# Moving first-layer weights and sums by one 64-byte line, and the attention products to between high and low parts

## The chip, the cores and the metric

The kernel runs on one core of one Trainium2 chip. The time is device microseconds of one execution; a profile is one further execution, recorded by the hardware profiler.

## The reference

Four batches of eight heads of attention over 768 positions with 64 elements each. A query sees the 8 first positions and the 96 before it, with a slope per head times the distance as bias. The result, 3072 rows of 512, goes through a layer of 2048 and back:

```python
scores = scale * np.matmul(q, k.transpose(0, 1, 3, 2)) + bias
a = softmax(np.where(keep, scores, -1e9))
x = np.matmul(a, v).transpose(0, 2, 1, 3).reshape(B * S, H * D)
h = x @ w_in                                    # 512 -> 2048
g = np.where(h > 0, h, np.exp(np.minimum(h, 0)) - 1)
return g @ w_out                                # 2048 -> 512
```

`w_in` and `w_out` come as 64-bit numbers.

## The kernel before, in words

The 3072 rows are taken as 12 groups of 256. Every number of the two layers is held as a high and a low part in the type fp32r, and a product is made of three: high by high, high by low, low by high. Weights are turned from 64-bit words into such parts once (`weight`), and stay in SBUF: `w0..` are the first layer's, `w1..` the second's, 16 pieces of 4096 bytes in a partition each. The inputs of a group are `xh` and `xl`, two pieces each.

Groups 0 to 2 go through the layers in four turns of four pieces while the weights arrive, group 3 in one turn (`moe`, lines 842 to 926). There an *up* of a piece is 12 matmuls of 256 columns (line 856; the weights are the stationary operand, the inputs the moving one), and a *down* is six of 512 columns (line 885; the values `gh`, `gl` are stationary, the second-layer weights move).

Groups 4 to 11 go through `seven` (lines 699 to 840). It takes two pieces together as a round: 24 up matmuls (line 713), and instead of eight products of quarter matrices in the down seven, by Strassen's scheme in Winograd's form: 21 matmuls of 256 columns (line 769). Three of the seven use values as they are, the *parts* `rh` (high) and `rl` (low); four use differences, the *sums* `sh` and `sl`. They are stationary; second-layer weights move, or mixtures of them (`mix`) that `prepare` made and stored in DRAM and that each round loads again. The down of a round is put into the plan as four pieces (`put`): parts with `rh` (6 matmuls), parts with `rl` (3), and the sums in two.

The attention of groups 3 to 11 is made by *visits* (`visit`, lines 614 to 640), four in each group for two heads each. One visit gives TensorE two things in one piece: products of weights and values of the visit two before (`values`, line 611, 48 matmul records) and the scores of a new one (`scores`, line 475, 16 records). Between them softmax runs on VectorE and ScalarE, and the transposed weights go through DRAM.

The order of the instructions of each engine is made by a planner (`Plan.order`): of what is ready it takes the smallest due time. `build` gives every piece its due time; rounds follow each other by 2 x `STEP`. `visit` passes a slack, `LATER`, by which the planner holds it back behind its operands. Addresses come from the order in which tiles are first asked for: `places_in_sbuf` asks for all places of the pool `m` in the order of `PLACES`, and weights get theirs in the pool `w` in the order in which the plan first loads them.

Of the kernel before, what the change touches and what calls it, by code (L numbers as in the profile page):

```python
# [8 lines left out]
F32 = mybir.dt.float32  # L9
# [7 lines left out]
P = 128  # L17
NG = 8
NL = P - NG
NT = 2  # L20
# [193 lines left out]
def act(n, psum=False, extra=0.0):  # L214
    return (("ACT", (55 if psum else 97) + 0.834 * n + extra, False),)


def dve(n, fast=False, port=False):
    return (("DVE", (75 + 0.521 * n) if fast else (70 + 1.042 * n), fast or port),)


def pool(n, two=True):
    return (("POOL", (30 + 2.58 * n) if two else (50 + 1.1 * n), True),)


def sp():
    return (("SP", 450.0, False),)
# [19 lines left out]
class Kernel:  # L247
# [366 lines left out]
    def visit(self, k, due):  # L614


        nc, p, N = self.nc, self.plan, len(self.fars)
        reads, cost = [], 250.0
        new = old = None
        if k < N:  # L620
            new = self.far(*self.fars[k][:-2], due, *self.fars[k][-2:])
            self.open.append(new[2])
            reads += [new[0]]
            cost += 575.0
        if k >= self.BEHIND:
            old = self.open[k - self.BEHIND]
            reads += old[0]
            cost += 640.0
        ss = [self.bank("s", "s", [P, NT, 2 * P]) for _ in range(2)]

        def both(e):
            if old:
                self.values(old[0], ss)
            if new:
                self.scores(new[0], ss, range(NT))

        p.add((("PE", cost, False),), both, reads, ss, due, slack=self.LATER)
        after = self.seat(old, ss) if old else ()
        if new:
            new[1](ss, after)  # L640
# [58 lines left out]
    def seven(self, rows, xh, xl, dues, step, last):  # L699

        nc, p, M = self.nc, self.plan, self.DM // 2
# [86 lines left out]
        for j in range(self.NFC // 2):  # L788
            d = dues[2 * j]
# [2 lines left out]
            combine(j, d + 2 * step)  # L792
            down(j, d + 3.7 * step)
        end = dues[self.NFC - 1] + 3 * step
        ob = [self.sb("io", "ob", [P, 2, M], slots=None if last else ["io0", "io1"]) for _ in range(NT)]
        lo, hi = ob
        P_ = lambda n: acc[self.OF[last][n][0]]
        q = lambda n: lambda: P_(n).t[:, self.OF[last][n][1]]
# [12 lines left out]

        if last:
            one, four, both = (self.sb("e", x, [P, M]) for x in ("one", "four", "both"))
            ob += [self.sb("io", "ob", [P, 2, M])]
            end_ = ob[2]
            p.add(act(M, True), lambda e: nc.scalar.copy(one.t, q(1)()), [P_(1)], [one], end - 9000)
            p.add(act(M, True), lambda e: nc.scalar.copy(four.t, q(4)()), [P_(4)], [four], end - 8999)
            whole = lambda x: lambda: x.t
            add(hi, 0, whole(one), q(2), [one, P_(2)])
            store(1, 0)  # L820
            add(end_, 1, whole(one), q(6), [one, P_(6)])
            p.add(dve(M), lambda e: nc.vector.tensor_tensor(both.t, end_.t[:, 1], q(7)(), ALU.add), [end_, P_(7)], [both], end - 9000)
            right = add(lo, 1, whole(both), q(5), [both, P_(5)])
            p.add(pool(M), lambda e: nc.gpsimd.tensor_tensor(lo.t[:, 0], both.t, four.t, ALU.add), [both, four], [lo], end - 9000, beside=[right])
            store(0, None)
            add(end_, 1, o(end_, 1), q(5), [end_, P_(5)])
            add(end_, 1, o(end_, 1), q(3), [end_, P_(3)])
            store(1, 1, 2, True)
            return
# [12 lines left out]
    def moe(self, rows, xh, xl, f0, f1, dues, step, part, X, last):  # L842
        nc, p, NFC, ws = self.nc, self.plan, self.NFC, self.ws
# [54 lines left out]
        for i in range(NT):  # L898
            if f1 < NFC:
                a = acc[i][0][0]  # L900
                if f0 == 0 or resumed:

                    self.parted.append(p.add(act(self.DM, True), lambda e, i=i, a=a: self.copy(e, part[i].t, a.t), [a], [part[i]], end - 9000))
                else:
                    p.add(dve(self.DM), lambda e, i=i, a=a: nc.vector.tensor_tensor(part[i].t, a.t, part[i].t, ALU.add),
                          [a, part[i]], [part[i]], end - 9000)
                continue

            for c, (a, at) in enumerate(acc[i]):
                n = at.stop - at.start  # L910
                ob = self.sb("io", "ob", [P, n], slots=None if last else ["io0", "io1"])
                e = "DVE" if c + 1 < len(acc[i]) else "ACT"
                cost = act(n, True) if e == "ACT" else dve(n)
                if f0 == 0 or resumed:
                    p.add(cost, lambda e, ob=ob, a=a, n=n: self.copy(e, ob.t, a.t[:, :n]), [a], [ob], end - 9000)
                else:
                    p.add(dve(n), lambda e, i=i, ob=ob, a=a, at=at: nc.vector.tensor_tensor(ob.t, a.t, part[i].t[:, at], ALU.add),
                          [a, part[i]], [ob], end - 9000)
                queue = nc.scalar if c else nc.sync
                k = 2 if i == 0 and 0 <= rows // W - self.HALVED[0] < self.HALVED[1] else 1  # L920

                def store(e, i=i, ob=ob, at=at, queue=queue, k=k):
                    for r in range(0, P, P // k):
                        queue.dma_start(self.out[rows + i * P + r:rows + i * P + r + P // k, at], ob.t[r:r + P // k])

                p.add((("ACT", 450.0, False),) if queue is nc.scalar else sp(), store, [ob], [], end, nbytes=P * n * 4)

    def places(self, n, x, c):

        if n == self.NE:  # L930
            return [self.THIRD[x + c]]
        return [f"{x}{n if n < self.NE else n % 2 ^ 1}{c}"]

    def build(self):
# [7 lines left out]
        at, start, wdue, dues = self.T0, {}, {}, []  # L942
        first = {}
        for n, f0, f1 in segs:
            start.setdefault(n, at)
            d, at0 = {}, at
# [8 lines left out]
        for n, (b, gi) in enumerate(groups):  # L955
# [6 lines left out]
            for hp in range(self.NP):  # L962
                d = lo + (hp + 1) * (hi - lo) / self.NP
                if len(self.EARLY) <= n < 3:
                    d = start[n] - self.SOON[0] - (self.NP - 1 - hp) * self.SOON[1]
# [5 lines left out]
        for far in soon:  # L971
            todo.append((min(far[-2], start[far[0] * self.GB + far[1]] - 1.0), lambda far=far: self.soon(far)))
        for k in range(len(self.fars) + self.BEHIND):
            d = self.fars[max(0, k - self.BEHIND)][-2] - max(0, self.BEHIND - k) * self.AHEAD
            todo.append((d, lambda k=k, d=d: self.visit(k, d)))
        for fc, d in wdue.items():
            for which in range(2):
# [15 lines left out]
        for j in range(NFC // 2):  # L993
            d = [x for (n, _, _), x in zip(segs, dues) if n == self.SE - 1][-1][2 * j + 1] + 2 * self.STEP
# [3 lines left out]
        for _, f in sorted(todo, key=lambda x: x[0]):  # L998
# [4 lines left out]

    LATE, FIRST_LOADS = 12, 22
    RESUMED = 4
    PLACES = (("pa0", 2048), ("pa1", 2048), ("pa2", 2048), ("pa3", 2048), ("pa4", 2048), ("pa5", 2048), ("qk0", 2496), ("xh0a", 2048), ("xh0b", 2048),
# [5 lines left out]
    PREPARE, SE = (168000.0, 9000.0, 6000.0), 4  # L1012
    OF = ({1: (0, 0), 2: (0, 1), 6: (1, 0), 5: (1, 1), 3: (2, 0), 7: (2, 1), 4: (3, 0)}, {1: (0, 0), 4: (0, 1), 6: (1, 0), 7: (2, 0), 2: (3, 0), 5: (4, 0), 3: (5, 0)})
# [16 lines left out]
    NEAR = {}  # L1030
    WARM = True
    WIDE, BEHIND_UP = ["h0", "h1", "v0", "t0"], 3.0
    THIRD = {"xha": "x0", "xhb": "ph2", "xla": "rk0", "xlb": "va0"}
    SLOTS = {"qk": ["rqv0", "qk0"], "v": ["va1", "va2"], "u": ["rk0", "va0"], "s": ["s0", "s1"], "t": ["t0"], "pv": ["v0", "t0"], "h": ["h0", "h1"], "o0": ["o0"], "o1": ["o1"],
             "pr": ["pr0", "pr1", "pr2", "pr3"], "tr": ["pt0", "pt1"], "pt4": ["ph0", "ph1"], "dd": [f"dd{i}" for i in range(4)], "st": [f"st{i}" for i in range(6)], "pt": ["pt0", "pt1"],
             "x": ["x0"], **{x + c: [f"{x}{n}{c}" for n in range(3)] for x in ("xh", "xl") for c in "ab"}, "e": ["e0", "e1"], "gh": ["gh0", "gh1", "gh2"],
             "gl": ["gl0", "gl1", "gl2"], "io": ["io0", "io1", "io2", "io3"], "part": [f"pa{i}" for i in range(6)], "mix": [f"pa{i}" for i in range(6)],  "hl": ["xh0a", "xh0b"], "tf": ["tf0", "tf1", "xl0a", "xl0b"],
             "g": ["io2", "io3"], "sum7": ["ph2", "x0"], "rh": ["gh0", "gh1"], "rl": ["gl0", "gl1"], "sh": ["xh2a", "xl2a"], "sl": ["xh2b", "xl2b"], "o2": ["v0"], "o3": ["t0"], "o4": ["s0"], "o5": ["s1"]}

    SOONER = {  # L1040
# [73 lines left out]

    def places_in_sbuf(self):
        for tag, size in self.PLACES:
            self.m.tile([P, size // 4], F32, tag=tag, name=self.n("place"))

    def gate(self, op):

# [249 lines left out]
```

## Time and profile before

| | us |
|---|---|
| median of 3 runs (lowest, highest) | 635.47 (634.56, 636.06) |
| the profiled execution | 634.52 |
| its span, first to last instruction | 632.7 |
| TensorE busy in it | 621.9 |

The span is what the trace shows; 1.8 us of the profiled execution lie around it. Busy TensorE is not TensorE at its peak: matmuls overlap, so the pace is read from pieces of a known number of matmuls in the chain of waits, which gives each piece the time until the next one ends.

### The profile page before, as it was taken

Reading aid. Unit: us, or ns where it says so; the run is one execution under the profiler, and the core shown is the slowest. Engines: PE = TensorE matmul, PEld = TensorE weight load, DVE = VectorE, ACT = ScalarE, POOL = GpSimd, SP = SyncE. Lnnn points to the kernel's source line nnn. Section 1 sums busy time; section 2 is a strip of 40 time slices with the busy share of each in tenths; the row PEclk is TensorE's granted clock in tenths of the full one; section 3 lists DMA queues with packets and bytes.
Section 4 is the critical chain, followed back from the end, with each engine's and each line's share of the span. In section 5 each row is a group of like instructions: output and inputs, shape, how many; then the busy total and the mean of one; then the engine's idle time right before and its main releaser. Section 6 shows DMA issues by size and latency. Waiting matters only on the chain.

```text
span 632.7 us, 19150 instructions
## 1 busy us (share of the span) xinstructions
PE 621.9 (98%) x7046; PEld 576.7 (91%) x7046; DVE 487.8 (77%) x1630; ACT 428.3 (68%) x1246; POOL 207.7 (33%) x491
## 2 busy tenths in 40 slices
PE   8999999999999999999999999999999999999995
PEld 5778888898898889999999999999999999999995
DVE  6899888878786877777877877877877877875755
ACT  5999778888656755667667667667667666655552
POOL 3645465656464784112112112112112112110000
PEclk9999999999999999999999999999999999999999
DMA  8979835322354899998898898998997997994542
GB/s 306 383 274 408 318 129 137 114 68 88 89 199 155 268 301 271 304 273 266 280 271 252 266 272 276 280 272 259 274 276 249 279 282 250 261 247 153 183 151 87
DMA packets 131171, 149.82 MB, mean 237 GB/s; under 512 B 63616, under 2 KB 82816, under 8 KB 131072
## 3 DMA queue, kind: packets, MB, share of 16 engines
q1 hardware_dynamic: 130784, 148.41, 74.9%
q8 instruction: 57, 0.93, 0.6%
q14 instruction: 42, 0.34, 0.2%
q10 hardware_dynamic: 288, 0.13, 0.1%
HBM read 117.57 MB, written 30.93 MB: 235 GB/s over the span
## 4 chain that ended last, share of the span: by engine, by line
PE 92%; DVE 3%; ACT 2%; issue 1%; DMA 1%; POOL 0%; ACTq 0%; DVEq 0%; POOLq 0%
PE h L713 28%; PE o L769 25%; PE h L856 13%; PE o L885 13%; PE s L611 5%; PE s L475 4%; PE pv L508 2%; PE t L528 1%; PE t L530 1%; DMA n_raw<-in_n_dram 1%; PE none L1141 1%; ACT pt L304 0%; ACT pr L465 0%; DVE g L397 0%; DVE hl L673 0%
## 5 line engine op out<-in xcount | busy, mean ns | idle before, releaser
L581 POOL TENSOR_SCALAR pr<-pr,st 128x168 f32<-128x168 f32 x144 | 74.1, 515 | 254.0 <-DVE st L483 197.5
L713 PE MATMUL h<-xh,w 128*128 128x256 f32 x1024 | 138.8, 278 | 0.0
L713 PEld LDWEIGHTS h<-xh,w 128*128 128x128 f32 x1024 | 127.7, 188 | 0.3
L723 DVE SCALAR_TENSOR_TENSOR gg<-e,h 128x256 f32<-128x256 f32 x128 | 53.6, 418 | 83.6 <-ACT e L722 83.5
L465 ACT ACTIVATE pr<-pr,nmax 128x168 f32<-128x168 f32 x192 | 82.8, 432 | 25.0 <-DVE nmax L463 24.7
L856 PEld LDWEIGHTS h<-xh,w 128*128 128x128 f32 x512 | 76.0, 188 | 9.8 <-DVE gl L312 0.6
L721 ACT ACTIVATE e<-h 128x256 f32<-128x256 f32 x128 | 49.0, 383 | 52.3 <-PE h L713 52.3
L885 PE MATMUL o<-w,gh 128*128 128x512 f32 x256 | 80.4, 399 | 0.4 <-ACT o L304 0.4
L856 PE MATMUL h<-xh,w 128*128 128x256 f32 x512 | 80.2, 282 | 0.2 <-DVE gl L312 0.2
L713 PE MATMUL h<-xl,w 128*128 128x256 f32 x512 | 79.8, 278 | 0.0
L713 PEld LDWEIGHTS h<-xl,w 128*128 128x128 f32 x512 | 68.3, 188 | 0.5 <-issue 0.2
L312 POOL TENSOR_TENSOR w<-g,w 128x256 fp32r<-128x256 f32 x64 | 50.2, 807 | 41.2 <-ACT w L304 20.5
L304 ACT CAST sh<-sum 128x512 fp32r<-128x512 f32 x64 | 39.9, 623 | 34.2 <-DVE sum L737 34.2
L463 DVE CUSTOM_DVE_ANT_0 pr<-s,far 128x168 f32<-128x168 f32 x192 | 53.5, 321 | 2.3 <-PE s L475 0.8
L722 ACT ACTIVATE e<-e 128x256 f32<-128x256 f32 x128 | 53.3, 416 | 2.8
L304 ACT CAST rh<-gg 128x384 fp32r<-128x384 f32 x64 | 33.0, 515 | 27.7 <-DVE gg L723 27.6
L586 DVE STREAM_TRANSPOSE tr<-pr 128x192 f32<-128x192 f32 x144 | 51.2, 366 | 0.5 <-POOL pr L581 0.3
L769 PE MATMUL o<-mix,sh 128*128 128x256 f32 x256 | 51.1, 281 | 0.0
L769 PE MATMUL o<-w,sh 128*128 128x256 f32 x256 | 50.6, 287 | 0.0
L312 DVE TENSOR_TENSOR sl<-sum,sh 128x512 fp32r<-128x512 f32 x64 | 43.7, 682 | 7.1 <-ACT sh L304 7.1
L885 PEld LDWEIGHTS o<-w,gh 128*128 128x128 f32 x256 | 42.9, 189 | 6.6 <-ACT o L304 0.8
L885 PE MATMUL o<-w,gl 128*128 128x512 f32 x128 | 45.0, 396 | 0.0
(141 smaller groups left out, 1390.7 us busy)
## 6 DMA issues: line engine op xcount, KB each, us to landing
mix<-mixed SPq DMA_DIRECT2D x192, 256.0 KB, 3.8
qk<-in_qkv_dram SPq DMA_DIRECT2D x48, 312.0 KB, 4.0
v<-in_qkv_dram SPq DMA_DIRECT2D x36, 384.0 KB, 4.8
dd<-tr SPq DMA_DIRECT2D x36, 384.0 KB, 4.1
pt<-dd SPq DMA_DIRECT2D x72, 192.0 KB, 4.0
bits<-in_w_in_dram SPq DMA_DIRECT2D x16, 512.0 KB, 7.6
bits<-in_w_out_dram SPq DMA_DIRECT2D x16, 512.0 KB, 9.4
mixed<-mix SPq DMA_DIRECT2D x32, 256.0 KB, 3.7
```

Of the source, the lines that this page charges most:

```text
L304: self.nc.scalar.copy(out, x)
L312: self.on(e).tensor_tensor(out, x, y, ALU.subtract)
L463: first = p.add((("DVE", 85 + 1.042 * LW, False),), lambda e: nc.vector.tensor_tensor_reduce(x(), s.t[:, i, :LW], tab, -(2.0 ** -(h + 1)), ...
L465: p.add(act(LW, extra=200), lambda e: nc.scalar.activation(x(), x(), AF.Exp, bias=nm, scale=-1.0, accum_out=st.t[:, n, 0:1]), [pr], [pr, s ...
L581: nc.gpsimd.tensor_scalar(pr.t[:, :LW], pr.t[:, :LW], st.t[:, n, 3:4], 1.0, ALU.mult, ALU.mult)
L586: nc.vector.transpose(tr.t[:, :, i, j], pr.t.rearrange("p (b r) -> p b r", r=32))
L713: nc.tensor.matmul(h.t, w1.t[:, s, cc * P:(cc + 1) * P], self.chunk(x, cc), start=n == 0 and s == HI and cc == 0, stop=n == 1 and cc == se ...
L722: p.add(act(W), lambda e: nc.scalar.activation(ex.t, ex.t, AF.Exp, scale=-1.0), [ex], [ex], d - 8000)
L723: p.add(dve(W), lambda e: nc.vector.scalar_tensor_tensor(gs(), ex.t, -1.0, h.t, ALU.add, ALU.max), [h, ex], [g], d - 8000)
L769: nc.tensor.matmul(acc[bank].t[:, half], a, b.t[:, LO if t == 1 else HI, x], start=j == 0 and t == 0 and n in first, stop=j == self.NFC // ...
L856: nc.tensor.matmul(h.t, w1.t[:, s, cc * P:(cc + 1) * P], self.chunk(x, cc), start=n == 0 and cc == 0, stop=n == 2 and cc == self.NCC - 1)
L885: nc.tensor.matmul(o.t[:, :at.stop - at.start], g.t[:, i * P:(i + 1) * P], w2.t[:, s, at], start=fc == f0 and n == 0 and s == HI and not r ...
```

## The change

Three things change. All weights are now asked for in `places_in_sbuf`, second-layer ones first, then a place of 64 bytes that nothing uses, then first-layer ones, then the other tiles in a new order. The sums move from `xh2`, `xl2` to `io0` to `io3`, and the values `gg` and the output tiles of the last part go the other way. With that the places start on other 64-byte lines; counted modulo four:

| operand | role in the matmul | line before | line after |
|---|---|---|---|
| first-layer weights `w0` | up, stationary | 2 | 3 |
| inputs `xh`, `xl` | up, moving | 1 | 2 |
| parts `rh`, `rl` (and `gh`, `gl`) | down, stationary | 1 | 1 |
| sums `sh`, `sl` | down, stationary | 1 | 3 |
| second-layer weights `w1` | down, moving | 2 | 2 |
| mixtures `mix` | down, moving | 2 | 2 |

All slices of these tiles that a matmul reads begin a multiple of 512 bytes from the start, so each keeps its tile's line.

Second, a visit whose values are for group 5 or later gets a due time counted back from the start of that group, two rounds from one visit to the next, half a unit behind the high parts of a down and half before the low ones. Third, such visits have a smaller slack.

```diff
@@ visit
-        p.add((("PE", cost, False),), both, reads, ss, due, slack=self.LATER)
+        p.add((("PE", cost, False),), both, reads, ss, due, slack=self.LATER if k < self.NP * 2 else self.LATER - 2500.0)
@@ seven
-        ob = [self.sb("io", "ob", [P, 2, M], slots=None if last else ["io0", "io1"]) for _ in range(NT)]
+        ob = [self.sb("io", "ob", [P, 2, M], slots=self.OUT + (["xh2a", "xl2a"] if last else [])) for _ in range(NT)]
...
-            ob += [self.sb("io", "ob", [P, 2, M])]
+            ob += [self.sb("io", "ob", [P, 2, M], slots=self.OUT + ["xh2a", "xl2a"])]
@@ moe
-                ob = self.sb("io", "ob", [P, n], slots=None if last else ["io0", "io1"])
+                ob = self.sb("io", "ob", [P, n], slots=self.OUT if f0 == 0 else ["io0", "io1"])
@@ build
         for k in range(len(self.fars) + self.BEHIND):
+            b, gi, hp = self.fars[max(0, k - self.BEHIND)][:3]
             d = self.fars[max(0, k - self.BEHIND)][-2] - max(0, self.BEHIND - k) * self.AHEAD
+            n = b * self.GB + gi
+            if n > self.SE:
+                d = start[n] - 2.3 * self.STEP + 0.5 - 4 * self.STEP * (self.NP - 1 - hp)
             todo.append((d, lambda k=k, d=d: self.visit(k, d)))
@@ the places
-    PLACES = (("pa0", 2048), ("pa1", 2048), ("pa2", 2048), ("pa3", 2048), ("pa4", 2048), ("pa5", 2048), ("qk0", 2496), ("xh0a", 2048), ("xh0b", 2048),
...
+    PLACES = (("w10", 4096), ("w11", 4096), ("w110", 4096), ("w111", 4096), ("w112", 4096), ("w113", 4096), ("w114", 4096), ("w115", 4096),
+             ("w12", 4096), ("w13", 4096), ("w14", 4096), ("w15", 4096), ("w16", 4096), ("w17", 4096), ("w18", 4096), ("w19", 4096), ("wline16", 64),
...
+    OUT = ["xh2b", "xl2b"]
...
-             "g": ["io2", "io3"], "sum7": ["ph2", "x0"], "rh": ["gh0", "gh1"], "rl": ["gl0", "gl1"], "sh": ["xh2a", "xl2a"], "sl": ["xh2b", "xl2b"], "o2": ["v0"], "o3": ["t0"], "o4": ["s0"], "o5": ["s1"]}
+             "g": ["xh2a", "xl2a"], "sum7": ["ph2", "x0"], "rh": ["gh0", "gh1"], "rl": ["gl0", "gl1"], "sh": ["io0", "io1"], "sl": ["io2", "io3"], "o2": ["v0"], "o3": ["t0"], "o4": ["s0"], "o5": ["s1"]}
@@ places_in_sbuf
-            self.m.tile([P, size // 4], F32, tag=tag, name=self.n("place"))
+            (self.w if tag[0] == "w" else self.m).tile([P, size // 4], F32, tag=tag, name=self.n("place"))
```

TensorE's order before, in `seven`, in front of the first products of a visit (the names are tiles, `s` the bank that a visit fills, `pt` and `v` its weights and values):

```order
L769 MATMUL o_7118<-w_113_982,rl_7086 128x256
L769 MATMUL o_7119<-mix_6956,rl_7086 128x256
L769 MATMUL o_7137<-mix_6987,sh_7082 128x256 x2
L769 MATMUL o_7137<-mix_6987,sl_7094 128x256
L769 MATMUL o_7137<-w_107_830,sh_7082 128x256 x2
L769 MATMUL o_7137<-w_107_830,sl_7094 128x256
L611 MATMUL s_7154<-pt_1322_7016,v_6750 64x64
```

Here the visit stands between the two puts of sums. The same place of TensorE's order now, in front of a visit:

```order
L713 MATMUL h_7281<-xl_6302,w_339_1454 128x256 x2
L713 MATMUL h_7281<-xl_6698,w_339_1454 128x256 x2
L769 MATMUL o_7203<-w_119_1170,rh_7250 128x256 x2
L769 MATMUL o_7203<-w_125_1261,rh_7250 128x256 x2
L769 MATMUL o_7204<-mix_7135,rh_7250 128x256 x2
L611 MATMUL s_7318<-pt_1334_7168,v_6920 64x64
```

It has moved from behind some of the sums to behind the high parts. And behind the visit, now:

```order
L475 MATMUL s_7319<-qk_6899 64x168
L769 MATMUL o_7203<-w_119_1170,rl_7269 128x256
L769 MATMUL o_7203<-w_125_1261,rl_7269 128x256
L769 MATMUL o_7204<-mix_7135,rl_7269 128x256
L769 MATMUL o_7226<-mix_7162,sh_7267 128x256 x2
L769 MATMUL o_7226<-mix_7162,sl_7277 128x256
L769 MATMUL o_7226<-w_119_1170,sh_7267 128x256 x2
```

The three matmuls of the low parts come first there, then all twelve of the sums; before, some or all of the sums were left.

## Rows read from the trace of the kernel before

**Rows 1.** The page, parts 1 and 2: busy time of the engines, and TensorE's granted clock.
```profile
PE 621.9 (98%) x7046; PEld 576.7 (91%) x7046; DVE 487.8 (77%) x1630; ACT 428.3 (68%) x1246; POOL 207.7 (33%) x491
...
PEclk9999999999999999999999999999999999999999
```

**Rows 2.** Busy time by stage: PE, PEld, DVE, ACT, POOL, clock, DMA share, GB/s.
```profile
75.00:245.00 170.00, 169.37 (x1542) 150.28 (x1541) 137.53 (x379) 123.58 (x354) 107.47 (x193) 1.00 0.53 165
245.00:620.00 375.00, 375.00 (x4611) 364.15 (x4610) 280.31 (x990) 237.63 (x680) 62.31 (x215) 1.00 0.85 255
```

**Rows 3.** Chain of waits, 410 to 470 us: start, length, engine, line, matmuls.
```profile
433.75 2.73 PE h L713 x24
436.48 2.38 PE o L769 x21
438.86 2.83 PE h L713 x24
441.69 2.47 PE o L769 x21
444.17 2.73 PE h L713 x24
446.90 1.70 PE o L769 x15
...
450.03 0.91 PE o L769 x6
450.94 2.73 PE h L713 x24
...
456.12 1.61 PE o L769 x12
457.74 2.73 PE h L713 x24
```

**Rows 4.** The same view, 254 to 272 us: visits at two other places.
```profile
255.03 0.68 PE o L769 x6
...
257.14 1.97 PE o L769 x15
259.11 2.73 PE h L713 x24
...
264.22 0.94 PE h L713 x8
...
266.60 2.04 PE h L713 x16
268.63 2.38 PE o L769 x21
```

**Rows 5.** Chain of waits, first and last of the slow pieces of 24.
```profile
271.02 2.83 PE h L713 x24
...
613.16 2.83 PE h L713 x24
```

**Rows 6.** Groups of instructions, shapes kept apart: form and count, busy us, mean ns.
```profile
L885 PE MATMUL o<-w,gh 128*128 128x512 f32 x256 | 80.4, 399 | 0.4 <-ACT o L304 0.4
L856 PE MATMUL h<-xh,w 128*128 128x256 f32 x512 | 80.2, 282 | 0.2 <-DVE gl L312 0.2
...
L885 PE MATMUL o<-w,gl 128*128 128x512 f32 x128 | 45.0, 396 | 0.0
L856 PE MATMUL h<-xl,w 128*128 128x256 f32 x256 | 40.4, 280 | 0.0
```

**Rows 7.** Chain of waits between 75 and 245 us.
```profile
88.55 1.83 PE o L885 x8
...
231.10 0.91 PE h L856 x8
...
232.93 0.47 PE h L856 x4
...
233.86 0.93 PE h L856 x8
```

11 rows, old and new, of the table PLACES are left out of this document.

## The prediction, made before the result was known

> **What bounds the kernel now.** [...] Busy time by stage shows where it is less than full: from 75 to 245 us it is busy 169.37 of 170 us, and from 245 to 620 us all of 375.00 [rows 2]. So in the long last stage no wait counts, and only the pace at which TensorE passes from one matmul to the next can change the time. What is left is before 75 us and in the last 12 us, where this change moves no instruction of TensorE.
>
> The chain of waits then gives that pace, and it shows two. In this stage the work comes in rounds: 24 up matmuls (line 713) and 21 down matmuls (line 769), all of one form, 256 columns. Some pieces of 24 take 2.73 us and others 2.83; pieces of 21 take 2.38 or 2.47 [rows 3]. Per matmul that is 113.6 ns against 117.8, a difference of 4.2 ns, with the same shape, clock and count and no idle time between them. I call them the fast and the slow rhythm. Three rules can be read from the same rows. First, the rhythm changes only at two kinds of place. Second, from a down piece to the next up piece it always changes over (2.38 then 2.83, 2.47 then 2.73), and from up to down it never does. Third, after attention products (lines 611 and 475) that stand inside a down piece the rest of that piece is slow: the 6 that follow take 0.91 us where 6 of the fast rhythm take 0.68 [rows 3, 4]. The slow tail of 6 then changes over into a fast piece of 24. One further case stands in the trace: attention products inside an up piece, after 8 of its 24; the 16 left take 2.04 us and the down piece after them is fast (2.38) [rows 4]. There the rhythm came out fast without a change-over.
>
> What do these places have in common? The up matmuls hold first-layer weights in the array and stream inputs; the down matmuls hold parts or sums and stream second-layer weights. By the addresses, both streams change their 64-byte line at each passage between up and down: weights start on line 2 of every four, inputs, parts and sums on line 1. In an up matmul the held operand is one line behind the streamed one (+1), in a down matmul one under (-1).
>
> [...]
>
> **The change part by part.** *The work.* TensorE gets the same instructions. Eight input scalings go from ScalarE to GpSimd and three subtractions from GpSimd to VectorE. From 245 us on, VectorE is busy 280 of 375 us, ScalarE 238 and GpSimd 62 [rows 2]; that cover hides these edits, and I cost them at nothing. Were the cover gone, they would show as idle time of TensorE, of which there is none now.
>
> *The lines.* After the change everything streamed starts on line 2 of four (inputs, second-layer weights, mixed weights), first-layer weights and sums on line 3, parts on line 1. So up matmuls and the 12 sum matmuls of a down piece are at +1, the 9 part matmuls at -1, and the parity of neither stream changes any more, at any passage.
>
> *What the rhythm costs now.* Slow in this stage are 17 up pieces of 24 (the first at 271.02, the last at 613.16), the 17 pieces of 21 behind them, and the tails after attention products: 18 of 6, 6 of 12 and one of 15 [rows 3 to 5]. 17 x 0.10 + 17 x 0.09 = 3.2 us, and (18 x 6 + 6 x 12 + 15) x 4.2 ns = 0.8 us. So the rhythm can give back 4.0 us here and no more. Of each 180 matmuls (four rounds, 23.99 us with two visits, 433.75 to 457.74 [rows 3]) 63 are slow.
>
> *The places of attention.* Visits now stand one and three rounds apart; after the change every two rounds, always after the 6 high-part matmuls of a down piece, with the 3 low-part matmuls behind. That place occurs once in the trace: 6 in 0.68 us, then the products, then 15 in 1.97 us, then a fast 2.73 [rows 4]. 15 of the fast rhythm take 1.70 [rows 3], so entry and slow tail cost 0.27, and 0.23 at the usual place (0.91 - 0.68). Taking away 4.2 ns for each slow matmul (0.06 and 0.03) leaves 0.20 to 0.21 for the entry at either. The number of visits stays, so moving them costs nothing by itself. A wait is not added: the values that a visit needs come from two visits before, after the change some 23.7 us earlier (twice two rounds of 5.11 us and 1.6 us of a visit); today one round and three together give 23.99 [rows 3]. What is queued behind a late visit would be the whole of TensorE.
>
> *Which rhythm follows.* No row has sums at +1 behind parts at -1. The bounds: every matmul of the stage slow costs 117 of each 180 x 4.2 ns = 0.49 us, some 16 times, 7.9 us more; every one fast gives 4.0 us. Within these I take what the nearest rows say: entry into parts at -1 is slow, as in all rows; passing from -1 to +1 turns slow into fast (0.91 or 1.97, then 2.73); at +1 the rhythm, once fast, stays so for 24 matmuls and more. What then happens where fast up matmuls at +1 pass to parts at -1 is bounded by nothing lost (the passage keeps the rhythm now) and all 9 part matmuls of each round slow: 64 rounds x 9 x 4.2 ns = 2.4 us. At the first end only 3 low-part matmuls after each of some 30 visits are slow, 0.4 us, and the stage gains 4.0 - 0.4 = 3.6; at the other it gains 4.0 - 2.4 = 1.6. The rows do not choose; I take 2.8, a little above the middle, since no passage from up to down in the rows loses the rhythm.
>
> *The stage from 75 to 245 us.* Up matmuls (line 856, 768 of them) and down matmuls of 512 columns (line 885, 384) [rows 6] stand mixed there, mostly 8 or fewer at a time, and the up ones have both rhythms as well: 4 in 0.47 us is 117.5 each, 8 in 0.91 is 113.8. Eight down ones take 1.83 us, 229 each [rows 7]; what the rhythm costs them I can't read from pieces so short, and I let the up ones stand for both. Here up stays at +1 and down at -1, only the change of parity goes. Where the pattern is regular, 4 of 12 up matmuls of a piece are slow [rows 7]. Taken for the whole stage, all fast would gain 768 x 4/12 x 4.2 ns = 1.1 us, and all slow would lose 768 x 8/12 x 4.2 ns = 2.2 us; no row lies nearer to one end than to the other; I take zero.
>
> **The sum.** 2.8 us less. The profiled execution took 634.52 us (632.7 of it the span, 1.8 around it), which becomes 631.7; it lies 0.95 us under the median of the runs, 635.47, so I forecast 632.7.
>
> **Rivals.**
> *The change-over goes on (slower).* The rhythm turns over once in every round whatever the lines, because it hangs on the passage itself, or because parts-to-sums takes the place of down-to-up as passage from -1 to +1. For it: in the rows it never fails, in either direction. Then visits every two rounds make it worse: slow after a visit, fast for one round (45), slow for the next (45). 90 of 180 slow instead of 63 is 27 x 4.2 ns = 0.113 us, 16 times 1.8 us: 637.3. It decides from the point where more than 35% of the matmuls are slow. Against it: the up piece after the visit at 264 came out fast without any passage [rows 4]. [...]
>
> *The slow rhythm is never left.* If only parity makes the change-over, it is gone, and every visit enters by the slow way: 7.9 us more, 643.4. For it: a tail after a visit stays slow for as long as 15 matmuls [rows 4]. Against it: today's -1 and +1 differ (one passage changes over, the other does not), which parity alone does not explain.
>
> *It gives and takes.* The last stage gains only 1.6 us and the stage before loses that much or up to 2.2: 635.5 to 636.1, no change that a measurement tells. For it: both ends are bounds of rows read above. Against it: the two would have to meet at their worst ends.
>
> **How the numbers follow.** The forecast (fast from the sums on) gets 0.47, its own range 630 to 634.3, from the two ends of the parts' price and half of the bounds of the stage before. The change-over that goes on gets 0.22, never leaving the slow rhythm 0.13, give and take 0.18. The range should hold eight in ten: from 629, the forecast with all parts fast and most of the gain of the stage before, up to 640, which takes in the change-over and a part of the way to the all-slow case, which is left out. About 0.2% (1.3 us) is what a measurement of this kernel can tell from no change. Faster by that: the forecast save its weak end, 0.45. Slower: the two slow cases, 0.34 of 0.35. Within: the rest, 0.21.
>
> **What would show it.** Right: in the chain of waits after 245 us, 24 up matmuls at 2.73 us nearly everywhere, no piece of 2.83, visits at equal distances, and TensorE busy without a gap. Pieces of 21 at 2.38 mean that parts keep the rhythm, about 2.42 that they lose it. Wrong: pieces of 2.73 and 2.83 in turn (the change-over goes on), or 2.83 throughout; or idle time of TensorE before line 611 (values late) or before line 713 at the start of a group, whose last visit now lies one round before it.

## The result, and the profile after

The changed kernel takes 642.47 us (median of 9 runs, 638.47 to 645.15) against 634.80 us (9 runs beside them, 634.39 to 636.06): ratio 1.0108, with a 95% interval from 1.0082 to 1.0134. It is slower, where 632.7 us was forecast, and outside the range that was given. The profiled execution took 641.95 us, 640.2 of it the span, 7.5 more than before.

Busy time first, from the page and by the same stages as [rows 1, 2] (PE, PEld, DVE, ACT, POOL, clock, DMA share, GB/s):

```profile
PE 624.8 (98%) x7046; PEld 577.3 (90%) x7046; DVE 489.4 (76%) x1633; ACT 427.6 (67%) x1238; POOL 200.0 (31%) x496
```
```profile
75.00:245.00 170.00, 169.35 (x1540) 149.44 (x1539) 137.92 (x384) 123.47 (x354) 105.21 (x191) 1.00 0.53 167
245.00:620.00 375.00, 370.48 (x4554) 358.32 (x4553) 277.57 (x977) 234.07 (x664) 57.04 (x222) 1.00 0.90 252
```

The stage from 75 to 245 us is as before, and the clock is full in both. From 245 us on TensorE, which had no gap there [rows 2], is idle for 4.5 of 375 us, and the share of the DMA engines rises from 0.85 to 0.90 while the rate falls from 255 to 252 GB/s. So the DMA engines are occupied longer for no more bytes.

What does TensorE wait for? The waits of TensorE name one tile that they did not name before (us in total, times, longest), and the view of that tile from 245 to 600 us has the time that its loads take from issue to landing:

```profile
PE s L611 <- DMA pt<-dd: 4.4, 9, 1.0
```
```profile
DMA to landing us min/median/max: 4.0/6.2/8.9
```

The same row of the kernel before reads:

```profile
DMA to landing us min/median/max: 3.2/4.1/7.4
```

`pt` holds the turned softmax weights, which go from SBUF to DRAM (`dd`) and come back in two loads (line 597). They take 2.1 us longer at the median, and TensorE stands still until some of them have landed. The chain of waits shows it at one place. Before, it ran over TensorE alone from 410 to 470 us [rows 3]; now it leaves TensorE (start, length, what):

```profile
508.94 4.24 DMA dd<-tr
...
514.19 7.23 DMA pt<-dd
...
521.56 0.86 PE s L611 x43
...
525.63 8.90 DMA pt<-dd
...
534.67 0.86 PE s L611 x43
...
536.16 1.92 PE o L769 x15
538.09 2.72 PE h L713 x24
540.81 2.38 PE o L769 x21
...
548.02 1.97 PE o L769 x15
549.99 2.83 PE h L713 x24
552.81 2.42 PE o L769 x21
555.23 2.72 PE h L713 x24
```

In these two visits 43 of the 48 products wait until the second load of `pt` has landed (521.56 and 534.67). The pieces from 548.02 on answer to [rows 3]. The visit ahead of them had nothing to wait for, and behind it the rhythm is slow for 15 down matmuls, 24 up matmuls (2.83) and the next 9 parts (2.42 instead of 2.38), then fast up to the next visit: 48 of 90 matmuls. From a down piece to an up piece the rhythm no longer turns over. Behind the late visit at 534.67 the pieces are fast at once. They are also fast behind nine others of the eleven late visits of this stage, and slow behind the one at 521.56.

How the 7.5 us add up: I take from the trace, for each line, the sum of the times from the start of an instruction to the start of the next one on TensorE. For lines 611 and 475 (visits) it grows from 61.6 to 68.8 us. For lines 713 and 769 (the rhythm) it falls from 337.9 to 337.3. For lines 856 and 885 (most of it from 75 to 245 us) it goes from 184.4 to 184.7. The visits cost 7.2 us, the rhythm gives back 0.6. What is left, about half a microsecond, lies in the first 75 us. In these sums a wait counts for the line that stands ahead of it: 1.2 us of the rhythm's 337.3 are TensorE waiting ahead of late visits. Without them the rhythm gives back 1.8 us, and it does so because late visits mostly leave the fast rhythm behind them: of 2880 matmuls of lines 713 and 769, 795 start 116 to 123 ns before the next one, against 1079 before.

### The profile page after: what moved, and what is told of

It reads as the page before. It is cut to its first block, busy times and chain, and to the rows that moved or that the text cites. A ratio compares the mean times of both kernels' runs of the same rounds, so it can differ in the third digit from the quotient of the medians.

```text
span 640.2 us, 19191 instructions
## 1 busy us (share of the span) xinstructions
PE 624.8 (98%) x7046; PEld 577.3 (90%) x7046; DVE 489.4 (76%) x1633; ACT 427.6 (67%) x1238; POOL 200.0 (31%) x496
## 5 line engine op out<-in xcount | busy, mean ns | idle before, releaser
L581 POOL TENSOR_SCALAR pr<-pr,st 128x168 f32<-128x168 f32 x144 | 66.0, 458 | 265.4 <-DVE st L483 259.2
L463 DVE CUSTOM_DVE_ANT_0 pr<-s,far 128x168 f32<-128x168 f32 x192 | 55.6, 326 | 4.6 <-ACT xh L304 2.1
L586 DVE STREAM_TRANSPOSE tr<-pr 128x192 f32<-128x192 f32 x144 | 48.9, 358 | 0.5 <-POOL pr L581 0.3
L769 PE MATMUL o<-w,sh 128*128 128x256 f32 x256 | 47.0, 277 | 0.0
```

What stands on the lines that cost most here:

```text
L463: first = p.add((("DVE", 85 + 1.042 * LW, False),), lambda e: nc.vector.tensor_tensor_reduce(x(), s.t[:, i, :LW], tab, -(2.0 ** -(h + 1)), ...
L581: nc.gpsimd.tensor_scalar(pr.t[:, :LW], pr.t[:, :LW], st.t[:, n, 3:4], 1.0, ALU.mult, ALU.mult)
L586: nc.vector.transpose(tr.t[:, :, i, j], pr.t.rearrange("p (b r) -> p b r", r=32))
L769: nc.tensor.matmul(acc[bank].t[:, half], a, b.t[:, LO if t == 1 else HI, x], start=j == 0 and t == 0 and n in first, stop=j == self.NFC // ...
```

## The experiments

Theory A: the lines do set where the rhythm turns, and the loss comes from the new places of the visits, which make `pt` late. The rivals: the lines themselves cost time, they are without effect, or `pt` is late for another reason. All results, with the sums of starts over the whole trace in us (each ratio is to runs of the kernel before taken beside that kernel, with medians from 634.80 to 635.23 us; waits ahead of a visit or inside a down piece stand in the rhythm's sum, in e7 some 11 us):

| kernel | median us | ratio to before (95%) | visits (611, 475) | rhythm (713, 769) |
|---|---|---|---|---|
| before | 634.80 | | 61.6 | 337.9 |
| changed | 642.47 | 1.0108 (1.0082 to 1.0134) | 68.8 | 337.3 |
| e1: new lines alone | 634.76 | 0.9993 (0.9983 to 1.0003) | 61.6 | 337.9 |
| e2: new visits alone | 645.56 | 1.0157 (1.0111 to 1.0202) | 69.2 | 339.7 |
| e5: changed, mixtures later | 635.81 | 1.0017 (1.0004 to 1.0030) | 61.6 | 338.1 |
| e7: e5, visits in the sums | 642.84 | 1.0090 (1.0060 to 1.0121) | 62.7 | 347.8 |
| e8: e5, visits ahead of the parts | 631.43 | 0.9938 (0.9922 to 0.9955) | 61.8 | 333.8 |
| e8b: e8, mixtures half as late | 631.76 | 0.9951 (0.9933 to 0.9970) | 61.6 | 333.9 |
| e9: e5, parts on line 3 | 634.63 | 0.9990 (0.9981 to 1.0000) | 61.5 | 337.8 |
| e10: e8 with the old lines | 636.35 | 1.0018 (1.0008 to 1.0028) | 62.3 | 339.2 |
| e11: visits ahead of the parts alone | 634.92 | 0.9992 (0.9979 to 1.0005) | 65.4 | 334.3 |

**e1 and e2: the two halves of the change.** e1 takes back the visits' rule, e2 the places:

```diff
# e1, from the changed kernel
-            if n > self.SE:
-                d = start[n] - 2.3 * self.STEP + 0.5 - 4 * self.STEP * (self.NP - 1 - hp)
...
-slack=self.LATER if k < self.NP * 2 else self.LATER - 2500.0)
+slack=self.LATER)
# e2, from the changed kernel (not printed): PLACES, the slots and places_in_sbuf of the kernel before
```

> The changed kernel with its places in SBUF, but the products of attention where they stood before (one and three rounds apart, inside the 12 sum matmuls or between parts and sums). Theory A (lines set the rhythm, the new places of attention make the loss): TensorE doesn't wait before line 611, whose starts sum to 27 us again; down-to-up passages no longer change the rhythm, so pieces of 24 at 2.73 us nearly everywhere and a time of 630.5 to 633 us. Theory B (the new lines themselves cost time, or the slow rhythm is not left after products inside the sums): pieces of 2.83 in many rounds, 637 us or more. Theory C (lines are without effect): as before, 634 to 636 us.

> The kernel before with its places in SBUF, and only the products of attention moved to every second round, after the 6 high-part matmuls. Theory A (the new places make the values late): TensorE waits before and inside line 611 for tile pt as in the changed kernel (starts of line 611 sum to 32 to 34 us against 27.2), and the rhythm changes over once a round with slow entry at each visit, so about half of the matmuls are slow: 641 to 644 us. Theory B (the layout makes the loss): 634 to 636 us, no wait before line 611.

e2 came out at 645.56 us, with the wait before line 611 (4.0 us in 6 waits) and 31 of 62 pieces of 24 slow, as theory A expected; its time lies 1.6 us above the range given. e1 came out at 634.76 without such a wait. The loss belongs to the visits; their due time and their smaller slack were not taken apart. But e1's time is not theory A's either: it is that of "lines are without effect". Its chain of waits shows that the new places have one:

```profile
307.05 2.72 PE h L713 x24
309.77 1.02 PE o L769 x9
...
312.23 1.61 PE o L769 x12
313.83 2.83 PE h L713 x24
316.66 2.42 PE o L769 x21
319.08 2.72 PE h L713 x24
321.80 2.38 PE o L769 x21
324.18 2.72 PE h L713 x24
```

No passage from down to up turns the rhythm (2.42 then 2.72, 2.38 then 2.72; before: 2.38 then 2.83 [rows 3]). The turn to fast has moved into the down piece: 2.42 is 9 slow parts and 12 fast sums. But a visit inside the sums does not go over into the fast rhythm, as theory A had it. Behind fast matmuls (1.02 for 9) it leaves the slow rhythm (1.61 for 12, then 2.83) until the next passage from parts to sums, up to 45 matmuls later (theory B's second reason, without its time). That the gain and the cost are equal, 337.9 us in both sums, is chance: they come from different matmuls.

**e5: the mixtures behind `pt`.** The planner's start of a load of mixed weights is put back by 3 us; TensorE's order stays, but for nine matmuls of one down piece.

```diff
# the ends of the two lines
-  [self.mixed[j][n]], [x], d - 6000 - 10 * n, nbytes=P * M * 8)
+  [self.mixed[j][n]], [x], d - 6000 - 10 * n, nbytes=P * M * 8, slack=10000.0)
```

> The changed kernel; only the planner takes the loads of mixed weights as able to start 3 us later after their place is free, so that SyncE issues the two loads of pt ahead of most of them; the order of TensorE stays. Theory A (pt is late because it queues behind loads of mixed weights): line 611 back to 27 to 28 us, landing of pt 4 to 5 us against 6.3, and 635.5 to 638 us (642.5 less 6.3 us, a little given back because visits that came late had started in the fast rhythm). Theory B (the scores, the softmax or the first store to memory make it late): line 611 stays above 32 us, 641 to 643 us.

635.81 us, no wait for `pt` before line 611, the visits' sum at 61.6 again. SyncE's issues show the difference. In the changed kernel, between the store of `dd` and the loads of `pt`:

```profile
508.94 0.37 SPq L590 DMA_DIRECT2D dd<-tr  x1
510.00 0.33 SPq L557 DMA_DIRECT2D v<-in_qkv_dram  x1
511.10 0.59 SPq L752 DMA_DIRECT2D mix<-mixed  x1
511.79 0.38 SPq L549 DMA_DIRECT2D qk<-in_qkv_dram  x1
512.26 0.86 SPq L752 DMA_DIRECT2D mix<-mixed  x2
513.26 1.50 SPq L597 DMA_DIRECT2D pt<-dd  x2
```

The same in e5:

```profile
503.22 0.37 SPq L590 DMA_DIRECT2D dd<-tr  x1
504.28 0.33 SPq L557 DMA_DIRECT2D v<-in_qkv_dram  x1
504.92 0.33 SPq L549 DMA_DIRECT2D qk<-in_qkv_dram  x1
507.86 1.28 SPq L597 DMA_DIRECT2D pt<-dd  x2
509.26 2.72 SPq L752 DMA_DIRECT2D mix<-mixed  x5
```

In the changed kernel three mixtures (256 KB each) and the loads of the visit (`v`, 384 KB, and `qk`, 312 KB) stand between the store and `pt`; in e5 the mixtures follow it here, and elsewhere mostly one of them or none is left ahead. But the mixtures are not what the change brought in. The kernel before issues three of them at this point too, at each of its 27 visits from 250 us on, and in 25 of these nothing else:

```profile
506.80 0.37 SPq L590 DMA_DIRECT2D dd<-tr  x1
509.48 1.68 SPq L752 DMA_DIRECT2D mix<-mixed  x3
511.29 1.31 SPq L597 DMA_DIRECT2D pt<-dd  x2
```

What came in is `v` and `qk`, which the new visits put there as well; taking the mixtures away makes up for it. From the issue of the store to the landing of the second load of `pt` the trace has 9.6 us at the median before, 12.7 in the changed kernel and 9.8 in e5. From that landing to the first product of the visit 2.8 to 5.5 us are left before, and 1.1 to 4.9 in e5; in the changed kernel it is 2.5 us at most, and the latest load lands 0.9 us after the visit has begun. The row of landings in e5:

```profile
DMA to landing us min/median/max: 3.3/5.0/7.9
```

That is not the 4.1 us of before, but it is enough. Theory A holds, with `v` and `qk` beside the mixtures: 6.7 us between the two medians (5.8 by the two ratios) are `pt` behind other loads. To put `v` and `qk` behind `pt` instead was not tried. How loads issued ahead of `pt` make it land later is not shown: the landings of the changed kernel and e5 (6.2 and 5.0 us) go with what is issued ahead of it, but before, `pt` stood behind three mixtures too and landed in 4.1.

**e7: visits in the sums.** e5 and `+ 2.5` for `+ 0.5` in the visits' due time, so that they stand after 6 of the 12 sums.

> As the one with later mixed weights, and the products of attention of every second round stand after 6 of the 12 sum matmuls (+1 line) instead of after the 6 high-part matmuls (-1). Theory A (entry at +1 goes over into the fast rhythm after a few matmuls and no passage is left that changes it): nearly all pieces of 24 take 2.73 us, no wait before line 611, 630.5 to 633 us. Theory B (each visit enters the slow rhythm wherever it stands, and it lasts for a round): 636 to 638 us.

642.84 us (639.06 to 646.39): both missed. The mixtures now came late, the first row of TensorE's waits:

```profile
PE o L769 <- DMA mix<-mixed: 7.8, 11, 2.0
```

For the rhythm only undisturbed visits count, and they do as in e1: slow behind the visit, through the 24 up matmuls (2.83) and the parts (2.42), then fast. The first half of theory A is refuted a second time: an entry at +1 is no better.

**e8, e8b, e10 and e11: visits ahead of the parts.** By what is left of theory A a visit should stand just ahead of parts, so that the passage to the sums comes 9 matmuls later. e8 is e5 with

```diff
-                d = start[n] - 2.3 * self.STEP + 0.5 - 4 * self.STEP * (self.NP - 1 - hp)
+                d = start[n] - 2.3 * self.STEP - 0.5 - 4 * self.STEP * (self.NP - 1 - hp)
```

e8b has `slack=5000.0` for the mixtures, e10 the places of the kernel before, e11 no slack for the mixtures.

> The changed kernel with later mixed weights, and the products of attention of every second round moved 6 matmuls ahead, to between the 24 up matmuls and the 9 part matmuls. Theory A (with the new lines only the passage from parts at -1 to sums at +1 turns slow into fast, and only a visit turns fast into slow): slow are just the 9 part matmuls behind each visit instead of 48 of each 90, so 39 x 4.3 ns x 29 visits = 4.9 us less than with later mixed weights alone (635.8): 630.5 to 632 us, and every piece of 24 at 2.72 us. Theory B (the slow rhythm lasts a whole round behind a visit, wherever it stands): 635 to 637 us.

> As e8, with the loads of mixed weights taken as 1.5 us later instead of 3 us. The order of TensorE is the same. Theory A: 630.5 to 632 us as e8, unless pt or the mixed weights come late in one of the two, which then shows as waits before line 611 or line 769. Theory B: 635 to 637 us.

> As e8, but with the places in SBUF of the kernel before. Theory A (the lines decide): each visit enters slow, every passage from down to up turns the rhythm over and none else does, so of each 90 matmuls 21 behind the visit and the second piece of 24 are slow, 45: 635 to 636.5 us. Theory B (the place of the visit alone gives the gain): 630.5 to 632 us.

> The changed kernel with the products of attention between the 24 up matmuls and the 9 part matmuls, the loads of mixed weights as the planner had them (up to three of them between the store of dd and the loads of pt). Theory A (two separate costs, the rhythm behind a visit and pt behind the mixed weights): the rhythm is as in e8, but pt is late again: starts of line 611 sum to 29 to 33 us against 27.4, landing of pt about 6 us, 633.5 to 638 us. Theory B (the place of the visit cures both): 631 to 632 us, no wait before line 611.

e8 took 631.43 us, 3.6 less than the kernel before beside it, and faster than both kernels of the change; e8b is as e8. Two rounds of its chain of waits, a visit right ahead of the first row:

```profile
346.57 2.62 PE o L769 x21
349.19 2.72 PE h L713 x24
351.91 2.38 PE o L769 x21
354.29 2.72 PE h L713 x24
```

All pieces of 24 are fast, and in none of its 62 does the trace show another. The same place with the old lines, e10:

```profile
348.12 2.67 PE o L769 x21
350.79 2.73 PE h L713 x24
353.52 2.38 PE o L769 x21
355.90 2.83 PE h L713 x24
```

Here all 21 behind the visit are slow, the passage from down to up turns to fast and the next one back to slow. e8 and e10 have the same order of TensorE's instructions and differ in the places in SBUF: 631.43 against 636.35 us, and the rhythm's sums differ by 5.4 us. That settles that the places act. Nearly every tile moved between the two, so that it is the 64-byte lines, and no other property of the addresses, is not settled by this pair; e9 moves less. e11 has e8's rhythm (334.3) and a late `pt` (3.0 us in 3 waits, visits 65.4): 634.92 us. The landing of one load hardly differs (5.6 us at the median, 5.5 in e8), but from the issue of the store to the last landing it is 11.5 us against 10.1. The two costs are separate and add up: 3.6 us for the visits and 0.5 for the rhythm are in the sums between e8 and e11, 3.5 in the medians.

**e9: parts on line 3.** A place of 128 bytes ahead of `gh0` puts the parts at +1, as all else, and moves `pt` and `v` of the visits by two lines too:

> The changed kernel with later mixed weights, and 128 bytes ahead of the places of the parts, which puts parts, as sums and first-layer weights, on line 3 (every matmul of the stage at +1; some tiles of attention move by two lines too). Theory A (the passage from -1 to +1 is what turns slow into fast): it is gone, so what a visit leaves lasts to the next visit, no change of rhythm between pieces without a visit; if every visit enters slow, all is slow, 640 to 642 us; if a visit turns the rhythm over, half is slow, 635 to 636.5 us. Theory B (it is the change from one kind of held tile to another, or the lapse of a round): the turn at the second passage into the sums stays, 635.8 us as with later mixed weights alone.

Between visits nothing turns any more, and each of 25 visits turns the rhythm over (the last two, without scores, leave it fast), which is theory A's second case; the time, 634.63, is 0.4 us under its lower end:

```profile
347.45 1.97 PE o L769 x15
349.41 2.83 PE h L713 x24
352.24 2.47 PE o L769 x21
354.71 2.83 PE h L713 x24
357.54 0.71 PE o L769 x6
...
359.68 1.91 PE o L769 x15
361.59 2.72 PE h L713 x24
364.31 2.38 PE o L769 x21
366.69 2.72 PE h L713 x24
```

Slow from 347 to the visit at 358, fast from there to the next. So the passage from -1 to +1 is what ends the slow rhythm in the changed kernel (2.42, then 2.72), and not the lapse of a round (2.47, then 2.83 here). That a visit turns it over in both directions may come from the parts or from the visits' own tiles, which moved too; the run does not tell these apart.

## Why the prediction was wrong

**The step that failed: "A wait is not added", and with it "moving them costs nothing by itself".** It compared the time from scores to values before and after (23.99 and 23.7 us) and took that for the whole matter. That time did stay (24.1 us in e5). What changed is what SyncE issues between `dd` and `pt`, where the visit's own loads came in beside the mixtures: `pt` took 6.2 us instead of 4.1, up to 8.9, and the visits took 7.2 us more, which is nearly all of the loss. The trace of before holds the time that `pt` had left, 2.8 to 5.5 us, but the prediction read no row of it; the step should have set it against the landing time, and it followed neither the issues of SyncE nor the load on the DMA engines. Its last sentence, that all of TensorE stands behind a late visit, was right. In "What would show it" I had named idle time before line 611, but gave it no chance in the sum.

**"Which rhythm follows", taken at a gain of 2.8, was mis-sized.** Without the wait (e5) the rhythm's sum is 338.1 against 337.9: no gain, where 2.8 us were forecast. Two of its three rules held: parts to sums turns slow into fast (2.42 us and then 2.72 in e1), and fast goes through parts without loss (2.38 between two pieces of 2.72 in e8). What failed is the length of the slow tail. I let it end with the 3 low-part matmuls behind a visit. In e5 and in the undisturbed visits of the changed kernel it lasts 48, since the passage to the sums right behind those 3 does not turn it; 9 matmuls behind a visit (e8) it does. Why 3 are too few is not shown. With the visit six matmuls earlier the sums fall by 4.2 us from e5 to e8 (338.06 to 333.84), where 4.9 was worked out from the same rules.

**"What the rhythm costs now", 4.0 us, held nearly**: e8 is 4.1 us under before in the rhythm's sum, though 9 of 90 matmuls are still slow, so that "no more" was some 1 us too low. About half of the excess lies in the fast pieces, which without a turn at their start take 2.72 us instead of 2.73; the rest was not placed. The tails of 6 are 20 and not 18 (the last two, of 0.90 us, stand behind visits without scores), which is 0.05 us. **The stage from 75 to 245 us at zero held** too, as a value between two bounds and not as one read from a row: 0.3 us more by the sums, 0.02 less busy.

**The rivals.** "The slow rhythm is never left" named 643.4 us, near the result, but that is luck, its mechanism is not there: of 62 pieces of 24 in the changed kernel 15 are slow. "The change-over goes on" is refuted by each passage from down to up after the change. "The lines are without effect", theory C of e1, is refuted by e8 against e10 (631.43 against 636.35 us) as far as the places go. What holds TensorE up by these 4.9 us is not shown.

## What to carry to other kernels

When a step is moved, follow its transfers on the issuing queue, and compare their landing time with the time left, before calling the move free; a constant distance between producer and consumer says nothing of what is issued in between. Where an engine has no idle time, a layout that takes away a cost must be timed together with the order of the work: here the new lines alone and the new visits alone gave nothing and a loss, and both, with the visits at another point and the mixtures later, gave 0.6%. When two edits come in one change, time each alone first.

## What the runs showed of the hardware that was not expected

- Back-to-back matmuls of 256 columns ran in two lasting rhythms here, 113.3 and 117.8 ns from start to start (2.72 and 2.83 us for 24). Which one ran depended on the places of the operands in SBUF (e8 against e10, 631.43 against 636.35 us) and on what ran before; read by 64-byte lines, the rows go as follows. With streams that keep their line, a passage from a pair at -1 to one at +1 ended the slow one (e8: 21 in 2.62 us behind a visit, then 24 in 2.72), and without such a passage each visit with scores turned it over (e9: 2.83 up to one visit, 2.72 behind it).
- With the old lines an entry was slow whether the matmuls before the visit were fast (the kernel before: 15 in 1.70 us, then 6 in 0.91 [rows 3]) or slow (e10: 24 in 2.83 us ahead of a visit, 21 in 2.67 behind one); the exceptions are one visit inside an up piece (16 in 2.04 us, then 21 in 2.38 [rows 4]), one of e10's two without scores, and one that began late (e2, with 4.0 us in 6 waits). With all pairs at +1 it depended on the state before (e9: 1.97 us for 15 behind fast matmuls, 1.91 behind slow ones).
- A short stop did what a visit did, in two places: in e8 at 586.4 us, with no visit there, the second part matmul starts 178 ns after the first instead of 113, and those behind it run at 117 to 120 ns. The same stands in e1 at 302.8 us (179 ns).
- In e9, with the values `gh`, `gl` on line 3 as well, the up matmuls of the stage from 75 to 245 us took 0.8 us less (starts of line 856: 92.1 us against 92.9 in e5). That was not followed up.
